# Attention rows kept in token order, routed by 16-byte records and gathered by number: one Trainium2 kernel, before and after

## The chip, the cores and the metric

The kernel runs on one core of one Trainium2 chip. A core has a tensor engine (PE, matrix products, which also transposes by a product with the identity), a vector engine (DVE), a scalar engine (ACT), GpSimd (POOL), SyncE (SP, which here only issues transfers) and 16 DMA engines that all queues share. The engines run side by side, each in its own fixed order, and wait for each other by semaphores. The metric is the device time of one execution in microseconds, taken over several runs.

## The reference, cut to what matters

Eight heads of eight sequences of 576 tokens attend within chunks of 64 tokens. The result, 4608 rows of 512 numbers, goes through a mixture of 8 experts: noisy logits choose two experts for each row, and both experts' outputs are added with softmax weights.

```
scores = scale * np.matmul(q_c, k_c.transpose(0, 1, 2, 4, 3))
attn = np.exp(scores - np.max(scores, axis=-1, keepdims=True))
attn = attn / (np.sum(attn, axis=-1, keepdims=True) + 1e-09)
x = np.matmul(attn, v_c)                      # (4608, 512) after a transpose
...
noisy_logits = x @ w_gate + np.log1p(np.exp(x @ w_noise)) * noise
top2 = np.argpartition(-noisy_logits, 2, axis=1)[:, :2]
for e in range(E):
    for k in range(2):
        mask = top2[:, k] == e
        h = np.maximum(x[mask] @ w1[e], 0.0)              # 512 -> 1024
        out[mask] += top2_w[mask, k, None] * (h @ w2[e])  # 1024 -> 512
```

## The kernel before, in words

**Attention.** 36 tiles of 128 tokens go through `attend(it)`, a software pipeline written out by hand: turn `it` issues the scores of tile it+1 (`scores`, L408), the product with V of tile it-2 (`pv`, L437), the transposes of tile it-1's probabilities (`p_trans`, L425) and of tile it-3's result (`x_trans`, L453), and for every fourth tile the gate's products (L465, L478). DVE takes the row maximum, subtracts it (`soft_max` L413, `soft_sub` L418), and divides (`norm_a` L442 adds 1e-9 to the sums, `norm_b` L445 takes the reciprocal, `norm_c` L448 multiplies). ACT does the exponential (L421) and the copies out of PSUM (`p_copy` L429, `x_copy` L459). q and k come in pairs of tiles into rings of three (`load_qk`, L325 and L326), v likewise (L331), all from SP but for the first pair of k, which ACT issues (L341).

**Routing.** `route(g)` takes a group of four tiles (the last group has eight). It is a generator: each `yield "dve"` ends a step, and `step_route("dve", 6)` takes six of them at the end of each turn, behind the turn's own work on DVE. At its end every token has two slot numbers (`lii`, L566), one in the list of each of its experts; PE contributes the ranks (L533, L535). `scatter` then has POOL write each tile twice to `slots` in DRAM by an indirect transfer (L600): 128 rows of 512 numbers and three more (a code of token and expert, and two weights), 2060 bytes each, from the tile `xs`. There are 72 such transfers, each behind a one-element copy on POOL (L598) that ties it to a place in the program.

**Experts.** Each expert has three blocks of three or four tiles of its list. `layer1` and `layer2` multiply in three split products (L231): high x high, high x low, low x high. Expert 0's three blocks are worked on while routing ends: their rows come from `slots` by SP (L170), and PE transposes them in `x_tile` (L214). `EARLY` says from which group on the first two blocks are complete. Later experts' tiles are loaded by SP straight from `slots` in four pieces each (L175) and transposed by DVE (L218). `resolve` turns a list's codes into row numbers and weights (nine DVE instructions, L151 to L159): `resolve_early` for a block of expert 0, `resolve_all` once for the rest, from lists loaded at L844. Outputs are added to `out` by indirect transfers from POOL (L198). `out` is cleared ahead by 37 tiles of zeros (`zero_out`, L670), and parts of `slots` by 9 more (L680, L682). Weights are loaded to `st` (L72, L75, L77) and split into high and low (`w_split`, L88 and L89).

**Order.** Nothing is scheduled by a program: instructions stand on each engine in the order in which the code above issues them. `hook_tail`, `hook1`, `hook2_f` and `hook2_r` are called between the expert layers' products, and put routing's last steps, the scatters and the next block's transposes there.

## Time and profile before

| | us |
|---|---|
| median of 3 runs (lowest to highest) | 995.22 (994.82 to 999.18) |
| the profiled execution, its own time | 993.54 |
| its span, from the first to the last instruction | 991.7 |
| mean granted clock of PE, share of full speed | 0.995 |
| DMA moved in the span | 132.92 MB |
| POOL's 72 routed writes, time on POOL | 72.5 |

All rows of the profile are from that one execution; times count from the span's start. In the views by group and of waits, a row names the engine, what it writes and reads (`PS<-kb,qb`), the source line (L408), and then busy or idle time in us, how often, and the longest or the mean. In the chain and in lists of single instructions the first number is the start and the second the length in us; in brackets stands how long the engine had been idle, and what ended that. The program falls into stages: loads to 13 us, turns without routing to 61, turns with routing to 150, the first expert block with the end of routing to 197, and then the experts.

### The profile page before, as it was taken

The numbers are of one execution on the slowest core, as the hardware profiler recorded it, in microseconds if no ns is written. First come the engines' busy times: TensorE is split into PE (matmuls) and PEld (weight loads), VectorE is DVE, ScalarE is ACT, GpSimd is POOL, SyncE is SP. The second block draws the span as 40 slices with busy tenths as digits, with TensorE's granted clock in tenths as the row PEclk, the third lists the DMA queues.
The fourth block names the chain that finished last, engine by engine and source line by source line (L and its number), as shares of the span: only waits on it lengthen the run. The fifth ranks groups of instructions, "written<-read, shape, count | busy, mean of one in ns | idle before, by whom it ended". The sixth has DMA issues, their size and how long they took to land.

```text
span 991.7 us, 16057 instructions
## 1 busy us (share of the span) xinstructions
PE 959.4 (97%) x5788; PEld 850.6 (86%) x5788; DVE 463.9 (47%) x1043; ACT 282.5 (28%) x595; POOL 225.8 (23%) x320
## 2 busy tenths in 40 slices
PE   6998988999999999999999999999999999999996
PEld 5886766898799888988998899889988998899885
DVE  6778774523445352544344434443344334433311
ACT  2565553222233221412231223132213221322100
POOL 3045556831100111121002101211111111111112
PEclk9999999999999999999999999999999999999999
DMA  8998899849611652166116622572264226402213
GB/s 300 317 368 285 293 376 395 268 143 149 180 33 33 154 136 37 33 142 149 35 28 136 159 48 28 112 178 44 32 154 133 44 32 154 112 12 32 33 22 44
DMA packets 97154, 132.92 MB, mean 134 GB/s; under 512 B 23440, under 2 KB 56592, under 8 KB 97072
## 3 DMA queue, kind: packets, MB, share of 16 engines
q1 hardware_dynamic: 80320, 93.02, 31.7%
q0 software_dynamic: 16432, 38.33, 19.3%
q8 instruction: 46, 0.75, 0.3%
q10 hardware_dynamic: 320, 0.52, 0.2%
q14 instruction: 36, 0.29, 0.1%
HBM read 81.69 MB, written 50.13 MB: 133 GB/s over the span
## 4 chain that ended last, share of the span: by engine, by line
PE 92%; DVE 4%; issue 2%; DMA 0%; POOL 0%; ACT 0%; another core or an unknown queue 0%; SPq 0%; DVEq 0%; POOLq 0%
PE PS L231 81%; PE PS L437 3%; PE PS L408 3%; PE PS L425 2%; PE PS L453 1%; PE PS L465 1%; PE PS L276 1%; DVE xs L448 1%; PE PS L478 1%; DMA kb<-in_kT 0%; POOL out L198 0%; DVE mx L413 0%; PE PS L214 0%; DVE pr L418 0%
## 5 line engine op out<-in xcount | busy, mean ns | idle before, releaser
L198 POOL DMA_INDIRECT out<-o,lid x77 | 119.9, 1557 | 662.0 <-DVE o L261 642.3
L231 PE MATMUL PS<-xh,w1h 128*128 128x384 f32 (+2 forms) x768 | 262.1, 341 | 4.8 <-issue 3.1
L231 PE MATMUL PS<-xl,w1h 128*128 128x384 f32 (+2 forms) x768 | 260.9, 340 | 0.2 <-DVE xl L222 0.2
L231 PE MATMUL PS<-xh,w1l 128*128 128x384 f32 (+2 forms) x768 | 260.9, 340 | 0.0
L250 ACT ACTIVATE hh<-PS 128x384 fp32r<-128x384 f32 (+2 forms) x192 | 95.2, 496 | 469.9 <-PE PS L231 421.3
L231 PE MATMUL PS<-w2h,hh 128*128 128x512 f32 x584 | 228.0, 390 | 0.0
L231 PE MATMUL PS<-w2h,hl 128*128 128x512 f32 x584 | 227.6, 390 | 0.0
L231 PE MATMUL PS<-w2l,hh 128*128 128x512 f32 x584 | 227.6, 390 | 0.0
L253 DVE SCALAR_TENSOR_TENSOR hl<-PS,hh 128x384 fp32r<-128x384 f32 (+2 forms) x192 | 108.6, 566 | 184.6 <-ACT hh L250 139.5
L261 DVE TENSOR_SCALAR o<-PS,lwt 128x512 f32<-128x512 f32 x77 | 57.7, 749 | 230.2 <-PE PS L231 222.9
L231 PEld LDWEIGHTS PS<-xh,w1h 128*128 128x128 f32 x768 | 144.5, 188 | 12.2 <-issue 8.2
L231 PEld LDWEIGHTS PS<-xl,w1h 128*128 128x128 f32 x768 | 144.6, 188 | 2.1 <-DVE xl L222 0.5
L231 PEld LDWEIGHTS PS<-xh,w1l 128*128 128x128 f32 x768 | 144.6, 188 | 1.0
L231 PEld LDWEIGHTS PS<-w2h,hl 128*128 128x128 f32 x584 | 109.2, 187 | 23.5
L231 PEld LDWEIGHTS PS<-w2h,hh 128*128 128x128 f32 x584 | 109.2, 187 | 22.5
L231 PEld LDWEIGHTS PS<-w2l,hh 128*128 128x128 f32 x584 | 109.2, 187 | 22.5
L600 POOL DMA_INDIRECT slots<-xs,lii x72 | 72.5, 1007 | 18.5 <-issue 17.9
L221 ACT ACTIVATE xh<-y 128x512 fp32r<-128x512 f32 x67 | 41.2, 614 | 92.6 <-DVE y L218 90.6
L222 DVE TENSOR_TENSOR xl<-y,xh 128x512 fp32r<-128x512 f32 x67 | 44.9, 671 | 48.2 <-ACT xh L221 45.4
L408 PE MATMUL PS<-kb,qb 128*64 128x128 f32 x576 | 43.2, 295 | 10.9 <-DMA kb<-in_kT 9.6
L408 PEld LDWEIGHTS PS<-kb,qb 128*64 128x64 f32 x576 | 34.0, 146 | 16.0 <-issue 13.0
L437 PE MATMUL PS<-vb,pts 128*64 128x130 f32 x576 | 40.2, 280 | 6.6 <-DVE gsm L543 1.7
(128 smaller groups left out, 701.2 us busy)
## 6 DMA issues: line engine op xcount, KB each, us to landing
st<-in_w SPq DMA_DIRECT2D x36, 512.0 KB
xg<-slots SPq DMA_DIRECT2D x252, 64.0 KB
st<-in_w SPq DMA_DIRECT2D x112, 128.0 KB
out<-zero SPq DMA_DIRECT2D x37, 256.0 KB
vb<-in_vh SPq DMA_DIRECT2D x36, 260.0 KB
qb<-in_qT SPq DMA_DIRECT2D x34, 256.0 KB
kb<-in_kT SPq DMA_DIRECT2D x34, 256.0 KB
xg<-slots SPq DMA_DIRECT2D x9, 256.0 KB
```

The lines of the kernel that those rows point to most:

```text
L198: s = nc.gpsimd.indirect_dma_start(out=out, out_offset=bass.IndirectOffsetOnAxis(ap=rows_of(i, j)[0:r], axis=0), in_=o[0:r], in_offset=Non ...
L221: nc.scalar.activation(oh, src, AF.Copy)
L222: nc.vector.tensor_sub(ol, src, oh.bitcast(FT))
L231: nc.tensor.matmul(p, a, b, start=first and n == 0, stop=last and n == 2)
L250: nc.scalar.activation(hh[:, 0:n], p, AF.Relu)
L253: nc.vector.scalar_tensor_tensor(hl[:, 0:n], p, 0.0, hh[:, 0:n].bitcast(FT), op0=OP.max, op1=OP.subtract)
L261: nc.vector.tensor_scalar(o[0:r], p[0:r], w, None, op0=OP.mult)
L276: nc.tensor.matmul(p[q * r:q * r + r], HR[0][:, f, 0:r], staged[e, 2, f // 2][:, (f % 2) * DM:(f % 2) * DM + DM], start=n == 0, stop=n == ...
L408: nc.tensor.matmul(PS[q, t % 2, hp * P:(hp + 1) * P], QB[t // 2][:, t % 2, hp, q], KB[t // 2 % RING][:, :, t % 2, hp, q], start=True, stop ...
L425: nc.tensor.transpose(PS[:, 2, hp * P:(hp + 1) * P], PR[t][:, hp * P:(hp + 1) * P], ident)
L437: nc.tensor.matmul(PS[q, 3 + hp // 2, o:o + 130], PT[t][:, hp, q], VB[t // 2 % RING][:, :, t % 2, c, hp, :], start=True, stop=True)
L600: s = nc.gpsimd.indirect_dma_start(out=slots, out_offset=bass.IndirectOffsetOnAxis(ap=lii[:, k, t0 + r:t0 + r + 1], axis=0), in_=XS[(t0 + ...
```

## The change

**Storage.** The attention result goes once, in token order, to `xbuf` (one store of four tiles every fourth turn, from SP). `slots` rows shrink to four numbers: `scatter` writes 16 bytes a row from a small tile `mt`. A list entry is thus only a number, and rows are fetched by it: `fetch_tile` has POOL gather 128 rows of `xbuf`. For expert 0 that is the tile PE transposes. For later experts the gathered tile is stored in order to `sorted_x` (`save`, SP) and loaded again by `load_tile` (SP, in four pieces, as before from `slots`). So a list must be resolved before its rows can be fetched: block 0's inside turn 33, block 1's in layer 2 of block 0, block 2's in layer 1 of block 1, the rest in layer 2 of block 1. The lists are now cleared by one transfer in turn 5.

**Turns.** `norm_a` moves from DVE to ACT, in front of `p_copy`, which moves in front of the exponential. Routing's maxima are taken two to a step, and the six DVE steps of a turn are split into three ahead of `norm_b` and three at the turn's end. `out` is cleared by one tile a turn from turn 14 on, two from turn 30 on, in place of eight in turn 32 and the rest later.

**Start.** q and k of the second pair are issued ahead of the first v, q by SP and k by ACT; the transposes of tile 0's probabilities go ahead of the scores of tile 2; constants that routing needs are made after turn 1 (`later_consts`).

```diff
...
-ROW = 576
-CODE, WA, WB, USED = DM, DM + 1, DM + 2, DM + 3
-CLEAN = max(CAPS) - P
+CODE, WA, WB, USED = range(4)
...
-    slots = dram.tile([LROWS * NE, ROW], FT, name="slots")
+    xbuf = dram.tile([NROWS, DM], FT, name="xbuf")
+    slots = dram.tile([LROWS * NE, 4], FT, name="slots")
     by_slot = slots.rearrange("(r e) c -> r e c", e=NE)
+    sorted_x = [[dram.tile([P, DM], FT, name=f"x{e}_{j}") for j in range(NLIST)] for e in range(NE)]
...
-    EARLY = {0: 3, 1: 6}
+    EARLY = {0: 3, 1: 6, 2: 7}
+    FETCH = 6
...
-    def gather_tile(i, k):
+    unsaved = []
+
+    def save(keep=0):
+        while len(unsaved) > keep:
+            e, j, r, x = unsaved.pop(0)
+            nc.sync.dma_start(sorted_x[e][j][0:r], x[0:r])
+
+    def fetch_tile(i, k):
+        save(1)
         e, b = BL[i]
         j, r = blocks[e][b][k]
-        n = rot["xg"] = rot["xg"] + (i >= NPE)
-        x = XG[e, j] = (later_xg[0] if n % 8 in (1, 2, 3) and i >= NPE else xg).tile([P, DM], FT, name="xg")
+        nc.gpsimd.memset(spacer, 0.0)
         if i < NPE:
-            d = nc.sync.dma_start(x[0:r], by_slot[j * P:j * P + r, 0, 0:DM])
-            if i in EARLY:
-                early_loads.append(d)
-            return
+            x = XG[e, j] = xg.tile([P, DM], FT, name="xg")
+            src = xbuf[0:P + sum(groups[EARLY[i]]) * P, :]
+        else:
+            x = later_xg[1].tile([P, DM], FT, name="xr")
+            src = xbuf
+            unsaved.append((e, j, r, x))
+        nc.gpsimd.indirect_dma_start(
+            out=x[0:r], out_offset=None, in_=src,
+            in_offset=bass.IndirectOffsetOnAxis(ap=rows_of(i, j)[0:r], axis=0))
+
+    def load_tile(i, k):
+        e, b = BL[i]
+        j, r = blocks[e][b][k]
+        n = rot["xg"] = rot["xg"] + 1
+        x = XG[e, j] = (later_xg[0] if n % 8 in (1, 2, 3) else xg).tile([P, DM], FT, name="xg")
         for q in range(4):
             nc.sync.dma_start(x[32 * q:32 * q + 32, 0:4 * r].rearrange("p (t c) -> p t c", c=P),
-                              by_slot[j * P:j * P + r, ds(place[e], 1), q * P:(q + 1) * P]
-                              .rearrange("(t p) o c -> p t (o c)", p=32))
+                              sorted_x[e][j][0:r, q * P:(q + 1) * P].rearrange("(t p) c -> p t c", p=32))
...
-
-
-    later = [(i, k) for i in range(4, NBL) for k in range(len(blocks[BL[i][0]][BL[i][1]]))]
-
-    ahead = [len(blocks[1][0])]
+            fetch_tile(i, k)
+
+
+    later = [(i, k) for i in range(NPE, NBL) for k in range(len(blocks[BL[i][0]][BL[i][1]]))]
+    to_fetch = list(later)
+
+    ahead = [0]
+
+    def fetch_more(most):
+        for _ in range(most):
+            if to_fetch and len(later) - len(to_fetch) < FETCH:
+                fetch_tile(*to_fetch.pop(0))
 
     def gather_more(most):
+        save()
         for _ in range(most):
+            fetch_more(1)
             if later and ahead[0] < LEAD:
-                gather_tile(*later.pop(0))
+                load_tile(*later.pop(0))
                 ahead[0] += 1
...
-    QB[0] = loads.tile([P, 2, 4, P], FT, name="qb", bufs=RING)
+    for j in range(2):
+        QB[j] = loads.tile([P, 2, 4, P], FT, name="qb", bufs=RING)
     for a in range(2):
         for h in range(2):
             nc.sync.dma_start(QB[0][h::2, a], qT[HALF[h], a])
             nc.scalar.dma_start(KB[0][h::2, h, a], kT[HALF[h], a])
+    for h in range(2):
+        nc.sync.dma_start(QB[1][h::2], qT[HALF[h], 2:4])
+        nc.scalar.dma_start(KB[1][h::2, h], kT[HALF[h], 2:4])
     nc.scalar.preload_act_table_set("natural_log_exp_and_others")
...
-    load_qk(1)
+    load_qk(2)
...
-        nc.vector.tensor_scalar(RC[t], pvb[:, :, :, 64:65], 1e-9, None, op0=OP.add)
+        nc.scalar.activation(RC[t], pvb[:, :, :, 64:65], AF.Identity, bias=eps)
...
         for r in range(G):
-            yield "dve"
+            if r % 2 == 0:
+                yield "dve"
             V.max(m[:, r], sp[:, r])
         for r in range(G):
-            yield "dve"
+            if r % 2 == 0:
+                yield "dve"
             V.max_index(mi[:, r], m[:, r], sp[:, r])
...
-        for x, s in parts:
-            yield "dve"
-            V.scalar_tensor_tensor(x.bitcast(I32)[:, :, CODE], mi[:, s, 0], 8192.0, tok[:, ts][:, s], op0=OP.mult, op1=OP.add)
+        yield "dve"
+        V.scalar_tensor_tensor(mt.bitcast(I32)[:, ts, CODE], mi[:, :, 0], 8192.0, tok[:, ts], op0=OP.mult, op1=OP.add)
...
-                in_=XS[(t0 + r) // 4][:, r % 4, 0:USED], in_offset=None)
+                in_=mt[:, t0 + r, :], in_offset=None)
...
-                    gather(i)
                     early_loads.append(nc.sync.dma_start(
                         meta0[i], by_slot[js * P:(js + m) * P, 0, CODE:USED].rearrange("(j p) c -> p j c", p=P)))
-            if g == LAST:
-                gather(len(EARLY))
+                    waiting.append((i, turn[0] + 2))
...
+    waiting = []
+    turn = [0]
+
+    def finish_waiting():
+        while waiting:
+            i = waiting.pop(0)[0]
+            resolve_early(i)
+            gather(i)
+
...
-        if it in (5, 7):
-            for r in range(CLEAN + 64 * (it // 2 - 2), CLEAN + 64 * (it // 2 - 1), 16):
-                nc.sync.dma_start(slots[r * NE:(r + 16) * NE, 0:USED], zero)
-        if it == 7:
-            nc.sync.dma_start(slots[(CLEAN + P) * NE:NLIST * P * NE, CODE:USED].rearrange("(p r) c -> p r c", p=P),
-                              zero[:, 0:3 * (NLIST * P - CLEAN - P) // 16].rearrange("p (r c) -> p r c", c=3))
+        if it == 5:
+            nc.sync.dma_start(slots[0:NLIST * P * NE].rearrange("(p r) c -> p (r c)", p=P), zero[:, 0:NLIST * NE * 4])
+            nc.sync.dma_start(xbuf[0:P], zero)
+        turn[0] = it
+        if waiting and it >= waiting[0][1]:
+            finish_waiting()
         if it in (9, 11, 13, 15):
             w_load(0, 1, (it - 9) // 2)
-        if it == 32:
-            zero_out(8)
+        if it >= 14:
+            zero_out(1 if it < 30 else 2)
         if it in (29, 31, 33, 35):
...
-        if it + 1 < NT:
+        if it <= 1:
+            p_trans(0) if it else scores(1)
+        if 0 < it < NT - 1:
             scores(it + 1)
...
-        if 0 <= it - 1 < NT:
+        if 0 < it - 1 < NT:
             p_trans(it - 1)
...
         step_route("pe")
+        if 0 <= it - 2 < NT:
+            norm_a(it - 2)
+        if 0 <= it - 1 < NT:
+            p_copy(it - 1)
         if it < NT:
             mx = soft_max(it)
             soft_sub(it, mx)
             scatter(1, mx[0:1, 0, 0:1])
             soft_exp(it)
-        if 0 <= it - 1 < NT:
-            p_copy(it - 1)
...
         step_route("act")
+        step_route("dve", STEPS // 2)
         if 0 <= it - 2 < NT:
-            norm_a(it - 2)
             norm_b(it - 2)
             scatter(1, RC[it - 2][0:1, 0, 0])
             norm_c(it - 2)
-        step_route("dve", STEPS)
-        if it > 32:
-            zero_out(3)
+            if (it - 2) % 4 == 3:
+                u = (it - 2) // 4
+                nc.sync.dma_start(xbuf[P + 4 * u * P:P + (4 * u + 4) * P].rearrange("(a p) c -> p a c", p=P), XS[u])
+        step_route("dve", STEPS // 2)
...
+        if it == 1:
+            later_consts()
...
+    finish_waiting()
...
-    TURNS = (((1, 7), (2, 3), (2, 6)), ((0, 6), (1, 2), (1, 6), (2, 2)))
+    TURNS = (((1, 7), (2, 3), (2, 6)), ((1, 2), (1, 6), (2, 2), (2, 6)))
...
+            if i == 1:
+                if f == 5:
+                    finish_waiting()
...
-            if f % 3 == 0:
+            if i == 0 and (k, f) == (0, 1):
+                finish_waiting()
+            if f % 2 == 0:
                 scatter(1)
+            if i == 1 and (k, f) == (0, 2):
+                resolve_all()
+            if i == 1 and k == 0 and f > 2 and f % 2:
+                fetch_more(2)
+            if i == 1 and (k == 1 and f % 4 == 3 or k == 2 and f % 2):
+                gather_more(1)
             if (k, f) in TURNS[i]:
                 x_tile(i + 1, TURNS[i].index((k, f)))
 
-        if 1 < i < NBL and i == 3:
-            resolve_all()
+        if i == 3:
...
-            resolve_early(0)
             layer2(0, hook2_r)
-        elif i == 1:
             finish_route()
             next_weights()
-            last_rows.close()
-            block_h(1)
             pg.close()
...
+            later_xg.append(pb.enter_context(tc.tile_pool(name="xr", bufs=3)))
...
-            gather(3)
...
-            resolve_early(1)
+        elif i == 1:
+            block_h(1)
...
```

Left out are: the constants' own lines, the paths for lists that overflow, and renames.

The order of instructions at three places follows. `x8` is eight in a row of the same kind; the tiles are named by the program. First PE's first rows: scores are L408 before and L442 after, the product with V is L437 and L471, the transposes of probabilities (`ident,pr`) are L425 and L459. Before:

```order
L408 MATMUL PS<-kb_108,qb 64x128 x16
L408 MATMUL PS<-kb_109,qb 64x128 x8
L425 MATMUL PS<-ident,pr 128x128 x4
L408 MATMUL PS<-kb_109,qb 64x128 x8
L437 MATMUL PS<-vb_111,pts 64x130 x8
L425 MATMUL PS<-ident,pr 128x128 x4
```

After:

```order
L442 MATMUL PS<-kb_193,qb 64x128 x16
L459 MATMUL PS<-ident,pr 128x128 x4
L442 MATMUL PS<-kb_194,qb 64x128 x16
L471 MATMUL PS<-vb_196,pts 64x130 x8
L459 MATMUL PS<-ident,pr 128x128 x4
```

The first transposes moved ahead of the scores of tile 2, the first that read the second pair of k (`kb_109`, now `kb_194`).

Second, ACT's first rows: transfers of k that ACT issues, the exponential (L421, now L455), the copy of transposed probabilities (L429, now L463), `norm_a` (L476) and the copy of the transposed result (L459, now L493). Before:

```order
L341 DMA kb_108<-in_kT 64x512 x4
L342 ACT_TABLE_LOAD
L421 ACTIVATE pr<-pr 128x512 x2
L429 ACTIVATE pts<-PS 128x512
L421 ACTIVATE pr<-pr 128x512
L429 ACTIVATE pts<-PS 128x512
L421 ACTIVATE pr<-pr 128x512
L429 ACTIVATE pts<-PS 128x512
L459 ACTIVATE xt<-PS 128x4x128
```

After:

```order
L367 DMA kb_193<-in_kT 64x512 x4
L370 DMA kb_194<-in_kT 64x1024 x2
L371 ACT_TABLE_LOAD
L455 ACTIVATE pr<-pr 128x512
L463 ACTIVATE pts<-PS 128x512
L455 ACTIVATE pr<-pr 128x512
L476 ACTIVATE rc<-PS,eps 128x8
L463 ACTIVATE pts<-PS 128x512
L455 ACTIVATE pr<-pr 128x512
```

ACT now issues two more transfers at the start; in each turn `norm_a` and the copy of the turn before stand ahead of the exponential.

Third, one turn of DVE with routing, from the row maximum (`mx`) on: the subtraction (`pr`), reciprocal and product (`rc`, `xs<-PS,rc`), and routing's steps, here the maxima and their indices (L516, L519 before; L550, L554 after). Before:

```order
L413 TENSOR_REDUCE mx<-PS 128x8
L418 TENSOR_TENSOR pr<-PS,mx 128x4x2x64
L442 TENSOR_SCALAR rc<-PS 128x8
L445 RECIPROCAL rc<-rc 128x8
L448 TENSOR_TENSOR xs<-PS,rc 128x512
L516 MAX gm<-gsp 128x8 x4
L519 MAX_INDEX gmi<-gm,gsp 128x8 x2
```

After:

```order
L447 TENSOR_REDUCE mx<-PS 128x8
L452 TENSOR_TENSOR pr<-PS,mx 128x4x2x64
L598 TENSOR_REDUCE lii<-gohr 128x2x4
L550 MAX gm<-gsp 128x8 x4
L479 RECIPROCAL rc<-rc 128x8
L482 TENSOR_TENSOR xs<-PS,rc 128x512
L554 MAX_INDEX gmi<-gm,gsp 128x8 x4
L558 TENSOR_TENSOR goh<-e_row,gmi 128x32
```

The addition L442 is gone from DVE, three steps of routing stand between the subtraction and the reciprocal, and three behind the product; with two maxima to a step these are ten instructions of routing where there were six.

57 lines of the change are left out of this document (29 added, 28 removed).

## The prediction

> **What bounds the kernel now.** I read the page's first lines, then the busy times by stage, then what the tensor engine (PE) waited for.
>
> ```profile
> span 991.7 us, 16057 instructions
> PE 959.4 (97%) x5788; PEld 850.6 (86%) x5788; DVE 463.9 (47%) x1043; ACT 282.5 (28%) x595; POOL 225.8 (23%) x320
> ...
> 0.00:13.30 13.30, 3.69 (x34) 3.35 (x34) 9.61 (x18) 2.54 (x3) 8.57 (x14) 1.00 0.73 229
> 13.30:60.90 47.60, 47.60 (x609) 40.70 (x613) 34.90 (x101) 25.89 (x54) 1.64 (x2) 1.00 0.98 352
> 60.90:126.60 65.70, 59.72 (x730) 48.10 (x732) 51.82 (x198) 36.01 (x82) 41.16 (x63) 0.97 0.89 301
> 126.60:150.50 23.90, 20.99 (x246) 16.94 (x246) 18.58 (x77) 13.19 (x28) 12.77 (x22) 1.00 1.02 382
> 150.50:197.00 46.50, 41.06 (x217) 34.65 (x215) 23.18 (x107) 12.90 (x29) 35.53 (x59) 0.96 0.94 329
> 197.00:983.40 786.40, 786.32 (x3967) 706.82 (x3967) 325.13 (x546) 192.00 (x399) 124.62 (x161) 1.00 0.41 87
> 983.40:991.70 8.30, 0.00 (x0) 0.00 (x0) 0.72 (x1) 0.00 (x0) 1.56 (x1) 0.77 0.24 34
> ```
>
> The rows give start and end, length, then busy us and instructions of PE, weight loads, DVE, ACT and POOL, the granted clock, the DMA share and GB/s. From 197 us on PE has no gap, and the change alters no matmul there; the last 8.3 us are the last output tile on its way out. So the kernel is bound by PE, and only what lies ahead of 197 us can be won: 9.6 us of idle before 13.3, 6.0 in 60.9 to 126.6, 2.9 to 150.5, 5.4 to 197. In the rows to 150 the DMA engines are nearly as full as PE, which the estimate has to respect.
>
> ```profile
> PE PS L408 <- DMA kb<-in_kT: 9.6, 2, 6.5
> PE PS L231 <- issue: 3.1, 3, 2.6
> ```
>
> **Part 1: the first loads and PE's first rows.**
>
> ```profile
> 1.97 2.50 ACTq L341 DMA_DIRECT2D kb<-in_kT  x4
> 6.47 3.68 PE L408 MATMUL PS<-kb,qb 128*64 128x128 f32 x32 [6.47 <-DMA kb<-in_kT]
> 8.28 0.59 SPq L326 DMA_DIRECT2D kb<-in_kT  x1
> 9.93 0.63 ACT L421 ACTIVATE pr<-pr 128x512 f32<-128x512 f32 x1 [4.15 <-DVE pr L418]
> 13.29 1.98 PE L408 MATMUL PS<-kb,qb 128*64 128x128 f32 x16 [3.14 <-DMA kb<-in_kT]
> 19.22 0.66 PE L425 MATMUL PS<-ident,pr 128*128 128x128 f32 x4
> ```
>
> PE does the scores of turns 0 and 1 until 10.15 and then waits 3.14 us for the second pair of K, whose last piece SP issued at 8.28, behind V. The change issues this pair straight behind the first, on SP and ACT: K then leaves at about 4.5 to 5.7 us. The first pair landed 2.0 us after its last issue (4.47 to 6.47), the second 4.4 us after (8.87 to 13.29). So the new landing lies between 7.7 and 10.1, before PE is free. PE also transposes turn 0's probabilities ahead of the scores of turn 2; that can run when the exponential ends (10.56). Scores of turn 2 then start at about 10.7 + 1.0 = 11.7 against 13.29 + 0: 1.6 us. The transposes that stood behind them (about 1 us) now fill the wait instead, so everything behind, the transposes at 19.22 first, comes about 2.6 us earlier. DVE's constants that moved behind turn 1 are short instructions in a stretch where DVE waits for PE. What is late next is V and DVE's work on turn 2. Ends: 0 (V, now behind 1 MB more, lands late) and 4.6 us, if the slow matmuls go too; I take **3**.
>
> ```profile
> 19.87 1.02 PE PS L408 x16
> ```
>
> Sixteen score matmuls take 1.98 us at 13.29 and 1.02 at 19.87: after the wait PE ran at about half rate for some 5 us. The Trainium skill (TensorE: Matmul & The Clock Gate, Part 1) says that PE starts at half rate and gets the full one after some 3.4 us of sustained work. The trace agrees in kind; by that rule PE, no longer stopped at 10.15, would be fast by turn 2, the term would be 4.6 and the sum 1.6 us better.
>
> **Part 2: the attention turns.** The same matmul group (four turns apart) in the chain of work:
>
> ```profile
> 33.52 1.00 PE PS L465 x8
> ...
> 60.91 1.00 PE PS L465 x8
> ...
> 126.59 1.00 PE PS L465 x8
> ```
>
> Two groups of turns without routing took 27.39 us, 13.7 each, with PE never idle; four groups with routing took 65.68, 16.4 each. Four times 13.7 is 54.8, so 10.9 us come on top, of which about 1.4 are rank matmuls that must be done; some **9.5** are loss.
>
> ```profile
> L442 DVE TENSOR_SCALAR rc<-PS 128x8 f32<-128x8 f32 x36 | 5.8, 162 | 20.3 <-PE PS L437 10.0 <-remote 3.7 <-PE PS L453 3.4
> 75.21 0.17 DVE L442 TENSOR_SCALAR rc<-PS 128x8 f32<-128x8 f32 x1 [1.62 <-remote]
> 76.48 2.00 PE L437 MATMUL PS<-vb,pts 128*64 128x130 f32 x16 [1.74 <-DVE gsm L543]
> 76.95 1.80 DVE L563 TENSOR_TENSOR xs<-gex,xs 128x4 f32<-128x4 f32 x1
> 77.45 1.27 POOL L89 TENSOR_TENSOR w1l<-st,w1h 128x512 fp32r<-128x512 f32 x1
> ```
>
> DVE is busy 51.8 of these 65.7 us and stands in order with PE, so both set the pace. The change takes the 162 ns instruction L442 off DVE (16 in this stretch: 2.6 us), issues the routing's maxima in pairs so that a group ends inside its four turns, splits DVE's six routing steps into three and three, and on ACT copies the transposed probabilities before the next exponential, so that PE's next product no longer stands behind DVE's subtraction. The cost: ACT does L442's work, 16 times about 0.2 us with 36.0 of 65.7 us busy, ahead of that copy. What stays: waits for something the trace cannot name (3.7 us in all) with a slow PE after them, and DVE instructions of 0.2 us that take 1.8 beside a POOL split. So I take **5** here, the shorter stretch to 150.5 included; ends 0 and 9.5 + 2.9.
>
> Against it stands one list that is now resolved inside turn 33:
>
> ```profile
> 181.95 0.16 DVE L151 TENSOR_SCALAR rsa<-meta 128x3 int32<-128x3 int32 x1
> ...
> 183.20 0.18 DVE L159 TENSOR_TENSOR lwt<-lwt,rsw 128x3 f32<-128x3 f32 x1
> ```
>
> These nine instructions took 1.43 us under PE's matmuls; in a turn that DVE paces they cost **1.4** at most, 0 at least. Their list is loaded two turns before, so DVE should not wait for it.
>
> **Part 3: bytes.** 32 routed writes of 128 rows x 2060 bytes in the stretch (8.4 MB) go; 16 tiles of x (4.2 MB) and about 16 tiles of zeros (4.2 MB, before this mostly behind 128 us) come. The bytes stay the 19.8 MB that 301 GB/s make, in some 5 us less: 326 GB/s. Before 60.9 the x stores add about 3.1 MB and the smaller clearing takes off 1.6: from 352 to some 384 GB/s, where the loads run four turns ahead.
>
> ```profile
> DMA packets 1608, 4.57 MB, mean 381 GB/s; under 512 B 297, under 2 KB 553, under 8 KB 1607
> ...
> DMA packets 703, 0.63 MB, mean 314 GB/s; under 512 B 425, under 2 KB 425, under 8 KB 702
> ...
> 36.81 0.69 SPq L682 DMA_DIRECT2D slots<-zero  x1
> ...
> q0 software_dynamic: 385, 1.28, 21.4%
> ```
>
> The first row (13 to 25 us) is what full engines move. The second (38.3 to 40.3) holds the 12-byte writes issued at 36.81: its large packets need 1.65 of the 2.0 us at 381 GB/s, so 0.35 x 16 / 425 = 13 ns for a small one. The last (60 to 75) has today's routed writes: 0.214 x 16 x 15 / 385 = 133 ns a packet. 9216 writes of 16 bytes cost 7.5 us of all engines at 13 ns and 77 us at 133. I take 13, the row nearest in size.
>
> **Part 4: 150 to 197 us**, routing's end between the first expert layers.
>
> ```profile
> 146.33 1.07 PE L214 MATMUL PS<-ident,xg 128*128 128x128 f32 x8
> 167.16 0.49 ACT L250 ACTIVATE hh<-PS 128x384 fp32r<-128x384 f32 x1 [4.12 <-PE PS L231]
> 168.30 0.44 PE L231 MATMUL PS<-xh,w1h 128*128 128x384 f32 x1 [2.61 <-issue]
> 168.83 0.52 PE L231 MATMUL PS<-xh,w1l 128*128 128x384 f32 x1
> 184.46 0.96 POOL L600 DMA_INDIRECT slots<-xs,lii  x1 [0.23 <-issue]
> 185.73 0.96 POOL L600 DMA_INDIRECT slots<-xs,lii  x1 [0.23 <-issue]
> ```
>
> Besides 5.4 us of idle, twelve matmuls after the 2.61 us gap ran some 0.32 us apart where neighbours are 0.17: 1.9 us, so 7.3 in all. 28 of the 37 zero tiles are issued in 140 to 175; most now go out earlier. Against it, expert 0's rows now come by gather: turn 33's list, three POOL gathers about 1.3 us apart (taken from L600's rows), 2 to 4.4 us to land: 1.4 + 3.9 + 4.4 = 10 us, with some 9 from turn 33's start (about 137) to the transposes at 146.33. So it fits barely; late it is 1 us of PE. Ends +7.3 and -4; I take **3**.
>
> **Part 5: the later experts.** Each tile is gathered (POOL), stored in order and loaded again (SP).
>
> ```profile
> 238.32 0.70 DVE L218 STREAM_TRANSPOSE y<-xg 128x512 f32<-128x512 f32 x1
> 243.16 0.70 DVE L218 STREAM_TRANSPOSE y<-xg 128x512 f32<-128x512 f32 x1
> ```
>
> Eight list loads took 8.93 us of SP (L844) and 16 weight loads as long; from lists complete near 203 I get lists on the chip at 219, numbers at 221, six gathers by 235, the first tile loaded at about 239.5 against 238.32. PE uses that block only after layer 2 of the one before, over 20 us later, and matmul outputs have four banks of 2.4 us. Cost **0**, at most about 7 once. Afterwards a tile is due every 786/77 = 10 us and the chain of a tile is two transfers longer; POOL, 125 of 786 us busy, has room.
>
> **Sum.** 993.54 (the profiled execution) - 3 - 5 + 1.4 - 3 = 983.9. That execution is 1.7 under the median of 995.22, by which it would be 985.6. I say **985**.
>
> **Rivals.**
> 1. *Full DMA engines take the turns' gain.* For it: a share of 0.98 before 60.9. Against: loads run ahead, and 381 GB/s was seen. Then parts 2 and 4 give nothing: 993.5 - 3 + 1.4 = 992. Chance 0.17.
> 2. *The first gather is late* and PE stops before layer 1, then runs slow: part 4 at -4, so 991. Chance 0.07.
> 3. *Slower: small routed writes cost as much as large ones*, on POOL's indexed path, which no row shows with rows this short. At 133 ns they need 77 us of all engines where today's need 72 x 3.2/7 = 33: 44 more, of which the free tenth of 60 to 150 takes 8, so 993.5 + 36 - 4 = 1025. It decides from about 70 ns a write (9216 x 70 / 16 = 40). Chance 0.13, for its milder forms too. The Trainium skill (DMA: Bandwidth & Descriptors, Specifications) speaks for this one: under 512 bytes a transfer does not reach line rate and becomes a read-modify-write. It gives no price; the 13 ns row speaks against a large one.
> 4. *The change does more*, with all of parts 1 and 2: under 974. Chance 0.05.
>
> My forecast, 977 to 990, has 0.58. A measurement of this kernel tells about 0.5% from no change, so faster means under 990.2. Faster: 0.58 + 0.05 + a quarter of rival 1 = 0.67; within 0.5%: 0.20; slower: 0.13. The range, 974 to 996, leaves out rivals 3 and 4.
>
> **What would show it.** Part 1: no wait for kb at 10 us, transposes near 16.5. Part 2: these groups under 15.3 us apart, no DVE row before the reciprocal, few PE waits for DVE. Part 3: small packets near 13 ns, DMA share under 0.95 to 126 us. Part 4: transposes of xg not after a gather, and no gap over 2 us behind them. Part 5: PE full from layer 1 of block 1 on. A PE gap after 190 us, or groups still 16 us apart, would prove me wrong.

## The result, and the profile after

The changed kernel takes 1007.45 us (median of four runs, 1005.69 to 1009.76) where the kernel before takes 995.25: a ratio of 1.0121, 95% interval 1.0093 to 1.0150. It is slower by 1.2%, against a prediction of 985. The profiled execution took 1005.69 us.

The first lines of the page of the changed kernel:

```profile
span 1003.9 us, 15872 instructions
PE 964.0 (96%) x5788; PEld 854.7 (85%) x5788; DVE 456.3 (45%) x1015; ACT 287.6 (29%) x631; POOL 309.6 (31%) x475
```

Its busy times by stage, with the columns and bounds of before:

```profile
0.00:13.30 13.30, 5.67 (x44) 4.67 (x46) 8.25 (x15) 2.55 (x4) 8.65 (x15) 1.00 0.78 264
13.30:60.90 47.60, 47.59 (x623) 40.24 (x621) 36.07 (x111) 29.21 (x70) 5.03 (x6) 1.00 1.00 365
60.90:126.60 65.70, 59.61 (x755) 49.12 (x752) 49.02 (x191) 39.43 (x102) 44.06 (x71) 1.00 1.01 352
126.60:150.50 23.90, 17.24 (x160) 13.61 (x158) 12.19 (x55) 9.44 (x26) 12.18 (x22) 0.79 0.91 301
150.50:197.00 46.50, 40.26 (x233) 34.42 (x233) 23.30 (x98) 14.13 (x33) 31.65 (x53) 0.96 0.23 70
197.00:983.40 786.40, 780.58 (x3934) 702.17 (x3933) 325.21 (x545) 192.82 (x401) 203.24 (x306) 0.99 0.53 127
```

PE's busy time is 4.6 us longer although it does the same matmuls, and between 126.6 and 150.5 the granted clock is 0.79 where it was 1.00: PE loses time twice, by standing and by running slowly after it. In 60.9 to 126.6 DVE has become lighter (51.82 to 49.02), but PE is no busier.

Where the 12.2 us of span come from is seen by following places of the program through the timeline of PE, first of the changed kernel, then of the kernel before: the gate products of turns 7, 31 and 35 (L499 and L465), the first x transposes (L240 and L214), and the first products of layer 1 of the first expert's second block (L257 and L231).

```profile
30.96 1.06 PE L499 MATMUL PS<-xt,wg 128*32 128x512 f32 x8
...
122.33 1.06 PE L499 MATMUL PS<-xt,wg 128*32 128x512 f32 x8
...
144.49 1.94 PE L499 MATMUL PS<-xt,wg 128*32 128x512 f32 x8
151.05 1.07 PE L240 MATMUL PS<-ident,xg 128*128 128x128 f32 x8
...
206.79 0.66 PE L257 MATMUL PS<-xh,w1h 128*128 128x384 f32 x1 [5.82 <-ACT xh L247]
```

The same in the kernel before, from the gate product of turn 31 on:

```profile
126.52 1.06 PE L465 MATMUL PS<-xt,wg 128*32 128x512 f32 x8
146.33 0.85 PE L214 MATMUL PS<-ident,xg 128*128 128x128 f32 x6
...
196.38 0.41 PE L231 MATMUL PS<-xh,w1h 128*128 128x384 f32 x1
```

The first gate product stands 2.5 us earlier than before (33.45 in the timeline), the one at the end of the routed turns 4.2 (126.52 to 122.33). The first x transposes are 4.7 us late (146.33 to 151.05): 8.9 us lost at the end of the turns. Layer 1 of the second block is 10.4 us late: 5.7 us lost on the way. The slow matmuls there add 2.6 more, so layer 2 of that block is 13.0 us late (213.59 to 226.63); from there to the last matmul nothing moves (983.33 to 996.41).

**The end of the turns.** The timelines of SP, POOL, DVE, ACT and PE of the changed kernel, turns 31 to 35:

```profile
119.83 4.47 SPq L709 DMA_DIRECT2D out<-zero  x4
...
122.84 0.98 POOL L632 DMA_INDIRECT slots<-mt,lii  x1 [0.45 <-issue]
...
128.13 0.39 SPq L646 DMA_DIRECT2D meta<-slots  x1
...
131.27 0.17 DVE L152 TENSOR_SCALAR rsa<-meta 128x3 int32<-128x3 int32 x1 [3.54 <-DMA meta<-slots]
...
134.08 1.46 PE L442 MATMUL PS<-kb,qb 128*64 128x128 f32 x16 [2.89 <-DVE pr L452]
141.13 0.27 ACT L476 ACTIVATE rc<-PS,eps 128x8 f32<-128x8 f32 x1 [5.86 <-remote]
142.56 2.00 PE L471 MATMUL PS<-vb,pts 128*64 128x130 f32 x16 [3.77 <-DVE xs L482]
```

The last routed write of the group is issued at 122.84, at a DMA share of 1.0, with zeros ahead of it. SP can issue the list's load only when it has landed (128.13), and the load takes 3.1 us more. DVE waits 3.54 us for it, and PE, in order with DVE, 2.89. One turn later ACT waits until 141.13, 5.86 us, for a signal of PE that comes late ("remote": the semaphore event lies behind the modelled end of the matmul that gives it), and PE stands 3.77. Sixteen products that take 1.1 us at the full clock take 2.0 behind that.

**The second block.** The timeline of PE and ACT shows the same kind of stop, with no wait for a transfer in it:

```profile
194.67 0.60 ACT L247 ACTIVATE xh<-PS 128x512 fp32r<-128x512 f32 x1 [10.42 <-PE PS L240]
200.36 0.60 ACT L247 ACTIVATE xh<-PS 128x512 fp32r<-128x512 f32 x1 [5.09 <-PE PS L240]
200.58 0.40 PE L257 MATMUL PS<-w2h,hl 128*128 128x512 f32 x1
206.05 0.60 ACT L247 ACTIVATE xh<-PS 128x512 fp32r<-128x512 f32 x1 [5.09 <-remote]
```

By the trace the transposes of the block's three tiles end at 194.56, 197.77 and 200.27; ACT starts on them at 194.67, 200.36 and 206.05, as PE's signals come at 194.60, 200.34 and 206.03. So the delay grows from nothing to 5.8 us while PE counts as busy. Whether PE itself was late or only its signal, the trace can't tell, because the ends of matmuls are modelled.

**The first block.** A third stop of this kind stands in layer 1 of the first block, 4.13 us in the changed kernel:

```profile
179.51 0.69 PE L257 MATMUL PS<-xh,w1h 128*128 128x384 f32 x1 [4.13 <-DVE hl L279]
```

The kernel before has it at the same place, in two pieces of 2.61 and 1.62 us (before 168.30 and 174.06).

### The profile page after: what moved, and what is told of

Same layout as the page of the kernel before. It is cut to its first block, busy times and chain, and to the rows that moved or that the text cites. A ratio compares the mean times of both kernels' runs of the same rounds, so it can differ in the third digit from the quotient of the medians.

```text
span 1003.9 us, 15872 instructions
## 1 busy us (share of the span) xinstructions
PE 964.0 (96%) x5788; PEld 854.7 (85%) x5788; DVE 456.3 (45%) x1015; ACT 287.6 (29%) x631; POOL 309.6 (31%) x475
## 5 line engine op out<-in xcount | busy, mean ns | idle before, releaser
L257 PE MATMUL PS<-xh,w1h 128*128 128x384 f32 (+2 forms) x768 | 263.4, 343 | 10.9 <-ACT xh L247 5.8
L257 PE MATMUL PS<-xl,w1h 128*128 128x384 f32 (+2 forms) x768 | 262.0, 341 | 0.0
L257 PE MATMUL PS<-xh,w1l 128*128 128x384 f32 (+2 forms) x768 | 261.8, 341 | 0.0
L257 PE MATMUL PS<-w2h,hh 128*128 128x512 f32 x584 | 227.9, 390 | 0.0
L257 PE MATMUL PS<-w2h,hl 128*128 128x512 f32 x584 | 227.6, 390 | 0.0
L257 PE MATMUL PS<-w2l,hh 128*128 128x512 f32 x584 | 227.6, 390 | 0.0
L257 PEld LDWEIGHTS PS<-xh,w1h 128*128 128x128 f32 x768 | 145.6, 190 | 18.6 <-POOL spacer L628 6.2
L257 PEld LDWEIGHTS PS<-xl,w1h 128*128 128x128 f32 x768 | 145.5, 189 | 2.2 <-DVE xl L248 0.4
L257 PEld LDWEIGHTS PS<-xh,w1l 128*128 128x128 f32 x768 | 145.4, 189 | 0.9
L257 PEld LDWEIGHTS PS<-w2h,hl 128*128 128x128 f32 x584 | 109.2, 187 | 23.4
L257 PEld LDWEIGHTS PS<-w2h,hh 128*128 128x128 f32 x584 | 109.2, 187 | 22.5
L257 PEld LDWEIGHTS PS<-w2l,hh 128*128 128x128 f32 x584 | 109.2, 187 | 22.4
L184 POOL DMA_INDIRECT xr<-xbuf,lid x67 | 66.4, 991 | 85.5 <-DMA x<-xr 69.8
L632 POOL DMA_INDIRECT slots<-mt,lii x72 | 71.5, 993 | 18.9 <-issue 17.2
L442 PE MATMUL PS<-kb,qb 128*64 128x128 f32 x576 | 42.8, 295 | 10.5 <-DMA kb<-in_kT 6.6
L471 PE MATMUL PS<-vb,pts 128*64 128x130 f32 x576 | 41.0, 284 | 9.4 <-DVE xs L482 5.4
```

The source lines that it names most:

```text
L184: nc.gpsimd.indirect_dma_start(out=x[0:r], out_offset=None, in_=src, in_offset=bass.IndirectOffsetOnAxis(ap=rows_of(i, j)[0:r], axis=0))
L257: nc.tensor.matmul(p, a, b, start=first and n == 0, stop=last and n == 2)
L442: nc.tensor.matmul(PS[q, t % 2, hp * P:(hp + 1) * P], QB[t // 2][:, t % 2, hp, q], KB[t // 2 % RING][:, :, t % 2, hp, q], start=True, stop ...
L471: nc.tensor.matmul(PS[q, 3 + hp // 2, o:o + 130], PT[t][:, hp, q], VB[t // 2 % RING][:, :, t % 2, c, hp, :], start=True, stop=True)
L632: s = nc.gpsimd.indirect_dma_start(out=slots, out_offset=bass.IndirectOffsetOnAxis(ap=lii[:, k, t0 + r:t0 + r + 1], axis=0), in_=mt[:, t0 ...
```

## The experiments

Each ratio is to the kernel before on the same chip, which took 982 us on two of the chips, 995 on one (and in the first pair) and 998 to 999 on two: the chips matter below.

**e1: the list one turn later** (changed kernel)

```
-  waiting.append((i, turn[0] + 2))
+  waiting.append((i, turn[0] + 3))
```

> The changed kernel, with block 0's list resolved one turn later (turn 34 in place of 33). Theory A (the loss between 128 and 155 us is the vector engine standing in turn 33 for a list that lands at 131.27): no wait of DVE for the list over 0.5 us, no PE gap of 2.9 and 3.8 us behind it, first x transposes for the experts at 143 us in place of 151.05, median 998 to 1000 against 1007.45. Theory B (moved clearing of the output fills the DMA engines, and whatever waits for a transfer here waits): the wait moves to the gathers or the weights, transposes stay at 149 to 151, median 1005 or more.

**e2: the zeros of the output where they were before** (changed kernel)

```
-  if it >= 14:
-      zero_out(1 if it < 30 else 2)
+  if it == 32:
+      zero_out(8)
...
+  if it > 32:
+      zero_out(3)
```

> The changed kernel, with the output cleared as before the change: eight tiles in turn 32, three a turn from 33, the rest behind. Theory A (place of the resolve): the list lands 1 to 2 us earlier at most, since the routed writes still have to land first; the DVE wait of 3.5 us shrinks to 1.5 to 2.5 and the median falls by 1 to 3, to 1004 to 1006. Theory B (DMA engines full from the moved zeros): the last routed write lands within 3 us of its issue in place of 4.8, the list within 2 in place of 3.1, the DVE wait is gone, DMA share in 60.9 to 126.6 falls from 1.01 to under 0.9, median 998 to 1000.

**e3: the first loads and PE's first rows alone** (kernel before)

```
+  nc.sync.dma_start(QB[1][h::2], qT[HALF[h], 2:4])
+  nc.scalar.dma_start(KB[1][h::2, h], kT[HALF[h], 2:4])
-  load_qk(1)
+  load_qk(2)
-  if it + 1 < NT:
+  if it <= 1:
+      p_trans(0) if it else scores(1)
+  if 0 < it < NT - 1:
```

> The kernel before with the change's start alone: second pair of q and k issued ahead of v, k by the scalar engine; transposes of tile 0 ahead of the scores of tile 2. Expected if the start acts alone: first gate product at 31.0 in place of 33.4 us, median 992.7 (2.5 less than before). Rival: loads so placed delay v and later turns, so that routing's turns give it back: 995.

**e4: the second block's transposes earlier** (changed kernel)

```
-  TURNS = (((1, 7), (2, 3), (2, 6)), ((1, 2), (1, 6), (2, 2), (2, 6)))
+  TURNS = (((1, 7), (2, 2), (2, 4)), ((1, 2), (1, 6), (2, 2), (2, 6)))
```

> The changed kernel, with the second and third tile of block 1 transposed earlier in layer 2 of block 0 (after steps 2 and 4 of the last tile in place of 3 and 6). Theory C (the stop of 5.8 us at 201 to 206.8 comes because PE runs dry right behind the third transposes, and PE's signal of them reaches the scalar engine late): the stop shrinks to under 1 us and the median falls by 6 to 8, to 1000. Theory D (the signal is late because of something that falls at 200 to 206 us, whatever PE does): the stop stays, median 1007. Theory E (PE waits for the gathered rows): the transposes start late, PE idles ahead of them, median 1007 or more.

Measured, on one chip where the kernel before takes 982.19: e1 992.24 (1.0092, 1.0073 to 1.0111), e2 985.06 (1.0025, 1.0011 to 1.0039), e3 979.15 (0.9968, 0.9953 to 0.9983), e4 991.96 (1.0091, 1.0074 to 1.0108). DVE's wait for the list in e1, by its timeline:

```profile
127.80 0.17 DVE L152 TENSOR_SCALAR rsa<-meta 128x3 int32<-128x3 int32 x1 [5.71 <-DMA meta<-slots]
```

The same in e4, and PE's wait behind it:

```profile
127.75 0.17 DVE L152 TENSOR_SCALAR rsa<-meta 128x3 int32<-128x3 int32 x1 [9.06 <-DMA meta<-slots]
...
130.55 1.97 PE L442 MATMUL PS<-kb,qb 128*64 128x128 f32 x16 [8.40 <-DVE pr L452]
```

And the waits of DVE in e2 (total, times, longest):

```profile
DVE rsa L152 <- DMA meta<-slots: 2.0, 1, 2.0
...
DVE y L244 <- DMA xg<-x: 8.9, 2, 8.5
```

On this chip the turns run ahead, and the list is waited for longer; a turn more (e1) does not reach it: its wait is shorter than e4's, but both end at 127.8. With the zeros out of its way the wait falls to 2.0 us, and e2 is 7 us faster than e1 and e4. What e2 has left shows against e3, which has the same start. The new turns win 1.6 us (54.9 against 56.5 for four groups), and the list takes it back: the first layer 1 begins at 137.3 and 137.2. The second block's layer 1 begins at 177.83 against 183.17, so part 4 does bring 5.3 us; e3 waits there 3.45 us for the block's rows from `slots`, e2 does not wait. But the first layer 1 of the next expert comes at 262.44 against 260.12: 7.7 us are gone again. The last row above shows where: DVE waits 8.5 us for the first later tile, which has to be gathered, stored and loaded, and PE stands behind DVE twice, 2.70 us before 209.74 and 2.75 before 235.61.

The busy times of e3 for its four routed groups, with the order of before on this chip:

```profile
57.19:113.72 56.53, 55.07 (x727) 46.84 (x725) 49.25 (x198) 36.44 (x82) 41.24 (x63) 1.00 1.00 375
```

PE is busy 55.1 of 56.5 us with the old order of DVE and ACT, where the same 727 matmuls took 65.7 us in the first profile; so the order of DVE, which I had taken for the pace, costs at most 1.5 us here. In all four profiles of this chip no signal of PE comes late up to the last matmul. In the first pair of profiles signals of PE lie up to 1.9 us behind in the kernel before, and more than 5 us in the changed one.

**b1, a1: both kernels again; e5: no wait left; e6: the start and the order of the turns alone.** b1 and a1 have no edit. e5 joins e1 and e2, lets the numbers of the later experts come nine steps of layer 2 later, and transposes the tiles of the next expert's first block a layer later (not shown):

```
+  if i == 1 and (k, f) == (1, 3):
+      resolve_all()
```

> The kernel before, unchanged, profiled beside the other runs. The turns with routing took 16.4 us a group in the first profile, where completions of PE reached other engines 1 to 3 us late in some seven places. If that was the kernel's own order (theory A), the groups are 16 us again; if it belongs to that execution or chip (theory B), they are 13.7 to 14 and PE idles under 2 us in the turns.

> The changed kernel, unchanged, profiled beside the other runs. If the list's wait in turn 33 is the loss wherever it runs, DVE waits 5 to 9 us at its first read of the list, PE stops behind it, and the ratio is 1.010 to 1.014. If the loss of the first profile came from late signals of PE, the ratio here is under 1.005.

> The changed kernel with the output cleared late, block 0's list resolved one turn later, all lists resolved in the second tile of layer 2 of block 1 (place 1,3 in place of 0,2), and block 3's tiles transposed during layer 2 of block 2 in place of layer 1. If the four waits are all that the change costs: no DVE wait over 1 us at a resolve, no PE gap over 1.5 us behind 130 us, ratio 0.995 to 0.997 as the start alone. If the gathers' chain (list, resolve, gather, store, load) is too long by itself: PE waits for block 2's or block 3's rows, ratio 1.000 or more.

e6 is e3 with the turns' edits, and without the storage in token order:

```
-  nc.vector.tensor_scalar(RC[t], pvb[:, :, :, 64:65], 1e-9, None, op0=OP.add)
+  nc.scalar.activation(RC[t], pvb[:, :, :, 64:65], AF.Identity, bias=eps)
...
+  norm_a(it - 2)
+  p_copy(it - 1)
...
-  step_route("dve", STEPS)
+  step_route("dve", STEPS // 2)
```

> The kernel before with the change's start and its order of the turns (addition on ACT, copy ahead of the exponential, maxima in pairs, three and three routing steps), without the new storage. If the turns are worth the 5 us that I took: ratio 0.991 to 0.993. If DVE never set their pace: 0.9965, equal to the start alone.

Measured on a chip with 995.28 before: b1 995.8, a1 1006.08 (1.011, 1.007 to 1.015), e5 1006.44 (1.0117, 1.0084 to 1.0151), e6 993.25 (0.998, 0.9956 to 1.0005). e5 has DVE's wait for the list gone and is no faster than a1. Rows of DVE, ACT and PE from its timeline:

```profile
135.88 0.16 DVE L152 TENSOR_SCALAR rsa<-meta 128x3 int32<-128x3 int32 x1
...
147.34 0.60 ACT L463 ACTIVATE pts<-PS 128x512 f32<-128x512 f32 x1 [2.73 <-remote]
...
147.99 1.53 PE L471 MATMUL PS<-vb,pts 128*64 128x130 f32 x16 [4.68 <-ACT pts L463]
```

A late signal of PE has taken the place of the wait. The stop at the second block is there again too (6.13 us before 207.18). In e6 four routed groups take 64.4 us, in b1 65.3: the new order in the turns is worth 0.9 us. b1, the kernel before, has no gather and no long stop at the second block, but the one in layer 1 of the first block is as long as those of the changed kernel. Rows of ACT and PE:

```profile
172.18 0.49 ACT L250 ACTIVATE hh<-PS 128x384 fp32r<-128x384 f32 x1 [6.20 <-remote]
...
173.31 0.69 PE L231 MATMUL PS<-xh,w1h 128*128 128x384 f32 x1 [4.62 <-DVE hl L253]
```

**e7: PE's instructions shifted; e2 again; e8: no zeros in turns 28 to 33; e9: transposes later in the kernel before.**

```
+  for _ in range(10):
+      nc.tensor.matmul(PS[:, 6, 0:16], jp, jp[:, 0:16], start=True, stop=True)
```

> The changed kernel with ten small matmuls of PE added at the start, in its wait for the first k, so that every later instruction of PE stands 20 places further on (a multiplication and a load of weights each); their result is overwritten. In the two profiles of the changed kernel PE's completions reached ACT 5 us late at 200 to 206 us, just where ACT needs the last transposes of block 1. Theory F (the late signals come at fixed places in PE's list of instructions): the stop there is gone or under 1.5 us and the late signals fall some 10 matmuls earlier in the program, ratio 1.003 to 1.007. Theory G (they come from what the other engines and transfers do at that time): the stop stays at 5 to 6 us, ratio 1.010 to 1.013. On a chip without late signals neither shows, and the ratio is that of the changed kernel.

> The same kernel as zeros late, once more. If clearing late is what helps wherever it runs: DVE waits under 2.5 us for the list, first transposes for the experts at most 1 us later than in the kernel before, ratio 1.001 to 1.004. If it helped only where PE's signals come in time: first transposes 5 us or more later than before, ratio 1.008 or more.

```
-  if it >= 14:
-      zero_out(1 if it < 30 else 2)
+  if 14 <= it < 28 or it >= 34:
+      zero_out(1 if it < 30 else 3)
```

> The changed kernel, with no tile of zeros issued in turns 28 to 33, three a turn from 34. Theory B1 (the transfers issued right ahead of the last routed writes and of the list delay the list): the list lands within 2.5 us of its issue in place of 3.1 to 5.3, DVE waits under 2.5 us, ratio 1.002 to 1.005. Theory B2 (what fills the DMA engines from turn 14 on has pushed loads back that are due later): no change, 1.009 to 1.012.

e9 is e3 with

```
-  TURNS = (((1, 7), (2, 3), (2, 6)), ((0, 6), (1, 2), (1, 6), (2, 2)))
+  TURNS = (((2, 3), (2, 5), (2, 6)), ((0, 6), (1, 2), (1, 6), (2, 2)))
```

> The kernel before with the change's start, and with block 1's tiles transposed later in layer 2 of block 0 (last tile, after steps 3, 5 and 6). The start alone had PE wait 3.4 us for the first of these rows, and ran slow for 6.8 us behind it. If that wait is all: no wait of PE for xg over 1 us there, ratio 0.990 to 0.993. If the rows come earlier than the transposes anyway (as in the first profile of the kernel before): 0.996 to 0.998.

Measured, with 998.44 before: e7 1013.15 (1.0172, 1.0122 to 1.0221), e2 again 1008.94 (1.013, 1.008 to 1.0181), e8 1009.62 (1.0132, 1.0083 to 1.018), e9 996.4 (0.9995, 0.9972 to 1.0018). e2's gain does not come again on this chip, though DVE's wait shrank to 1.31 us; the timelines of DVE, ACT and PE show why:

```profile
131.31 0.17 DVE L152 TENSOR_SCALAR rsa<-meta 128x3 int32<-128x3 int32 x1 [1.31 <-DMA meta<-slots]
...
141.32 0.27 ACT L476 ACTIVATE rc<-PS,eps 128x8 f32<-128x8 f32 x1 [6.02 <-remote]
142.76 2.00 PE L471 MATMUL PS<-vb,pts 128*64 128x130 f32 x16 [5.15 <-DVE xs L482]
```

e8, without zeros in those turns, has the same outcome: DVE waits 1.78 us for the list, and PE stands 5.06 us before 143.39. In e7 the stop at the second block stays at the same matmul (7.39 us before 210.73) though PE's instructions are shifted by the ten added. So it hangs on the place in the program and not on where an instruction lies in PE's stream. In e9, with plain reads and late transposes, a shorter stop of 2.40 us stands there, before 196.97.

**e10: the light writes alone** (kernel before; x is read from rows of `w2`, so its routing is left out)

```
-  in_=XS[(t0 + r) // 4][:, r % 4, 0:USED], in_offset=None)
+  in_=XS[(t0 + r) // 4][:, r % 4, CODE:USED], in_offset=None)
...
-  nc.sync.dma_start(x[0:r], by_slot[j * P:j * P + r, 0, 0:DM])
+  nc.sync.dma_start(x[0:r], w2[0, j % 8 * P:j % 8 * P + r, :])
```

> The kernel before, with routed writes of 12 bytes into a separate list in place of the 2060-byte rows; x of every block is read from other rows (of w2), in the same number and size, so routing of x is left out. The list of block 0 is loaded ahead of its x. Theory A (the late signals and the stop of 5 us at the first expert's second block come with the lighter routed writes, whose rows no longer fill the DMA queues between 150 and 200 us): the stop shows here, a PE gap of 4 to 7 us at the first layer1 of block 1, and the time is +4 to +8 us against the kernel before, if the start of the other parts is unchanged. Theory B (they come with the gathers by number): no stop over 2.5 us there, the time within -6 to +1 us. Theory C (they come with what stands in the program at that place, the transposes and the order): no stop either, since the order there is that of before.

**e11: plain reads in place of the gathers of the first expert** (changed kernel; which rows are read is left out)

```
+  if i < NPE:
+      nc.sync.dma_start(x[0:r], src[j * P:j * P + r])
+      return
   nc.gpsimd.indirect_dma_start(
```

> The changed kernel, with the x of the first expert's blocks read as whole rows by SP in place of the gathers by number on POOL; which rows is left out, so the output is not routed for that expert. Theory A (lighter writes): the stop of 4 to 7 us at layer1 of block 1 stays, the time within 1001 to 1010 us on a chip where the changed kernel takes 1006. Theory B (gathers): the stop is gone, 5 to 9 us less than the changed kernel. The list of block 0 is waited for by DVE as before the edit, some 3 to 4 us in turn 33 or 34, in all theories, but PE's wait there should not be shorter.

**e12: added traffic** (changed kernel, in layer 2 of the first block)

```
+  nc.sync.dma_start(copy[n * P:(n + 1) * P], xbuf[P + n * P:P + (n + 1) * P])
```

> The changed kernel with 36 copies of 256 KB within HBM issued by SP in the first expert's layer2 of block 0, two at each step, that nothing waits for, so that the DMA share between 150 and 200 us is that of the kernel before or more (0.6 to 1.0 in place of 0.23). Theory A (lighter traffic): the stop at layer1 of block 1 shrinks to under 2.5 us, 4 to 7 us less than the changed kernel unless the copies delay the weights of the next layers. Theories B and C: the stop stays at 4 to 7 us, time that of the changed kernel or some us longer by the copies.

**e13: e4 again**

> The kernel of e4 again (the transposes of block 1 stand at steps (1,7), (2,2), (2,4) of layer2 of block 0, two steps earlier), beside the others on this chip. Theory C (the late signals follow the place of the transposes just ahead of layer1, with too little work left behind them): with 16 more matmuls between the last transposes and layer1 (some 5.5 us of layer2) the wait of PE at layer1 of block 1 is under 2 us, and the time 4 to 7 us under the changed kernel's. Theory D (PE itself stands still there, and its signals are late for that): the stop of 4 to 7 us comes all the same, in that layer1 or ahead of it, time within 3 us of the changed kernel's.

Measured, with 999.04 before: e10 996.6 (0.9975, 0.9947 to 1.0003), e11 1009.61 (1.0109, 1.0065 to 1.0153), e12 1013.57 (1.0156, 1.0103 to 1.021), e13 1006.55 (1.0082, 1.0053 to 1.0112). e10 has no stop at the second block, so light writes alone do not bring that one; in layer 1 of the first block it has one of 4.83 us, as b1 has. e13 has the stop at the second block with more work behind the transposes (4.87 us before 206.98), so their place does not bring it either. e11 has neither the stop of turn 34 nor the one at the second block. Its timelines of ACT, SP and PE show the wait of ACT that was 5.86 us, and then a new wait that keeps its time long:

```profile
141.16 0.27 ACT L479 ACTIVATE rc<-PS,eps 128x8 f32<-128x8 f32 x1 [2.25 <-PE PS L474]
...
217.28 8.99 SPq L75 DMA_DIRECT2D st<-in_w  x16
226.38 3.11 SPq L185 DMA_DIRECT2D xg<-xbuf  x4
...
232.31 1.12 PE L243 MATMUL PS<-ident,xg 128*128 128x128 f32 x4 [6.86 <-DMA xg<-xbuf]
```

Layer 2 of the second block begins at 217.8 in e11 and at 226.6 in e13 on the same chip: 8.8 us less without gathers, 4.0 of it up to the first x transposes. They are lost again, since SP now has the third block's reads behind 16 weight loads. In e12 the stop at layer 1 is gone too, but PE stands 3.62 us ahead of the transposes at 199.03, and the copies delay what comes later: no answer on traffic.

**e14, e15: gathers, and the same bytes as plain reads, in the turns** (kernel before, turns 12, 18, 24 and 30)

```
+  if it in (12, 18, 24, 30):
+      read_spare()
...
+  nc.gpsimd.indirect_dma_start(
+      out=spare[:, a], out_offset=None, in_=w2.rearrange("e f n -> (e f) n"),
+      in_offset=bass.IndirectOffsetOnAxis(ap=rows3[:, a:a + 1], axis=0))
```

In e15 the last three lines are

```
+  nc.sync.dma_start(spare[:, a], w2.rearrange("e f n -> (e f) n")[a * P:(a + 1) * P])
```

> The kernel before with three gathers by number of 128 rows of 2 KB, from an input, into a spare tile at turns 12, 18, 24 and 30, twelve in all, which nothing reads. POOL has about 12 us more to do in 70 us. Theory B (a gather by number is followed, 5 to 15 us later, by a late completion signal of PE, and by that by a stop): after each of the four places a late signal of 2 to 6 us that the kernel before does not show there, and 8 to 20 us more in all. Theory E (gathers do nothing to PE by themselves; e11 lost the stop for another reason, such as the shifted times): late signals as in the kernel before, the time within -3 to +4 us, the 4 us for the added traffic and POOL's time.

> The same with plain reads of 128 rows of 2 KB by SP in place of the gathers, at the same four turns: the same bytes without POOL. Theories B and E both: no late signal that the kernel before does not show, the time within -2 to +4 us. What e14 takes longer than this run is the price of the gathers being by number.

Measured, with 982.25 before: e14 984.58 (1.0029, 1.0014 to 1.0044), e15 984.02 (1.002, 1.0011 to 1.003). Neither shows a late signal. But nor did any profile of the other chip with 982 us, gathers or not, so the pair says only that gathers do not delay PE on such a chip. For the others the question stays with e11.

## Why the prediction was wrong

At layer 2 of the second block the kernel should have been 9.6 us ahead by the terms, and it was 13.0 us behind. Of these 22.6 us the list makes 7.5 and the stage to 197 us 11.3.

- **Start, -3: right.** 2.6 us by the profile, with the transposes of before's 19.22 at 16.61 (16.5 forecast); e3 alone is 0.3% faster than before. The first rows of PE after:

```profile
9.61 1.98 PE L442 MATMUL PS<-kb,qb 128*64 128x128 f32 x16 [1.00 <-DVE mx L447]
...
12.56 3.24 PE L442 MATMUL PS<-kb,qb 128*64 128x128 f32 x32
...
17.20 1.09 PE L442 MATMUL PS<-kb,qb 128*64 128x128 f32 x16
```

  PE is slow at 9.61 and fast at 17.20; the rate changes within the row at 12.56, at 15.2 by the starts of its products. The Trainium skill (TensorE: Matmul & The Clock Gate, Part 1) has the full rate after some 3.4 us of sustained work; the trace has it later, 5.6 us after the 1.00 us pause and 8.6 after the first product, so the 4.6 us that I worked out beside it did not come.
- **Turns, -5: mis-sized, from a false reading.** They brought 1.7 us in the first pair, 0.9 by e6 against b1, and about 1.6 by e2 against e3. The 9.5 us of "loss" that I divided between DVE's steps are not DVE's pace: with the same order another chip takes 56.5 us for these four groups, 55.1 of them with PE busy (e3). On the chip of the first profile late signals of PE stand in the rows where time is lost; the "remote" 3.7 us were their trace, and I had filed them under what stays.
- **The list, +1.4: the first step that failed.** "Their list is loaded two turns before, so DVE should not wait for it" counted turns, not transfers. From the write's issue to the numbers went 8.4 us (122.84 to 131.27) at a DMA share of 1.0. On a chip with 982 us this explains most: 1.0091 with a wait of 9.06 us (e4), 1.0025 with 2.0 (e2). On the others it is not enough to take it away (e5, e2 again), since the late signal then stands in its place. In the first pair the end of the turns cost 8.9 us in place of 1.4: PE stood 2.89 us behind the list and 3.77 behind the late signal, and ran slowly after both.
- **Bytes: the price right, the share wrong.** Between 62 and 120 us the changed kernel's routed writes are the only traffic on their queue (packets, MB, share of 16 engines):

```profile
q0 software_dynamic: 864, 0.06, 1.1%
```

  0.011 x 16 x 58 / 864 gives 12 ns a packet, against 13 taken; POOL needs 990 ns to issue a write where it needed 997. But a packet is not a row, as I had counted it: 28 writes have 3584 rows and left 864 packets, by the trace half of 128 bytes (eight rows) and half of 4. So all 72 writes cost the engines some 1.6 us (0.64 x 72 / 28) and not 7.5. The rival with dear small writes falls, and e10 agrees. But I forecast a share under 0.95 in the turns, and it is 1.01 (0.89 before) at 352 GB/s where I had 326, and in this full stage the list was late.
- **150 to 197 us, -3: the largest miss, and the second step that failed.** I took the idle time there for the work of full DMA engines, which would go with the zeros. The DMA share fell from 0.94 to 0.23, and layer 1 of block 0 still took 27.7 us (27.8 before), with 4.13 of them a stop that no transfer explains; then the stop and the slow matmuls of block 1 cost 8.3. So the term came out at +8.3 in place of -3. In e11, one profile without gathers, the stop at block 1 is not there; why is open. On the first chip with 982 us, where e3's wait is one for rows, the term came out at -5.3 (e2 against e3).
- **Later experts, 0:** right in the first pair, where the late start may have covered the longer chain of a tile (not shown); on the chip with 982 us it cost 7.7 us, the "at most about 7 once" of the prediction, and took back what part 4 had won.
- **Rivals.** The first gather was not late for PE: its three transfers were issued from 132.43 on, and no wait stands before the transposes at 151.05. What was late was the list, for DVE. No rival had a stop of PE that no transfer explains.

What stays open: why PE's signals come late, and why only on some chips. A gather is not needed for it: the stop in layer 1 of the first block stands in every profile of those chips, in one or two pieces of 3.0 to 5.9 us together, without gathers too (4.62 us in b1, 4.83 in e10), and in none of the chips with 982 us. For the two long stops of the changed kernel it is shown that on the chips with 995 to 999 us both long stops stand in every profile of the changed kernel and its variants with gathers, the second in e12 in another form, and neither in e11 without gathers; whether that is the gathers, POOL's work for them or the shifted times, one profile does not tell. The late signal in turn 34 lets ACT go on 8.65 to 8.85 us after the first gather is issued in seven of eight of these profiles and 10.2 us in e5, where the gather stands 3 to 5 us later; that is a coincidence in time, not a mechanism. The version that beats both is the start alone (e3, 0.9968, 0.9953 to 0.9983, on the one chip where it ran).

## What to carry to other kernels

A load that depends on a write is due after the transfer times of both, behind all that is queued ahead of them; count microseconds at the DMA share of that stage, not turns. An idle time whose releaser the profile can't name is not to be credited to the engine beside it: look at a second profile, from another chip, before pricing its removal. And when a change moves traffic into a stage that is already full, ask which small transfer on the path to a wait stands behind it.

## What was not expected of the hardware

- Signals of PE reached ACT and DVE up to 5 us and more after PE's modelled end on the chips with 995 to 999 us, in the kernel before as well (up to 3.7 us in b1), and on neither chip with 982 us. The kernel before differs by 1.7% between chips (982 to 999), all of it early: from the next expert's first layer 1, at 273.4 us in the first profile and 260.1 in e3, both take 710 us to the last matmul.
- A stop of 3 to 6 us costs more than its length, since matmuls run at half clock behind it: around the second stop the granted clock is 0.50 from 202.9 to 213.2, and PE works again from 206.8 on, so 6.4 us of products were slow and 2.6 us were lost on top of the stop.
